# First head pair rotated on VectorE, float64 weight halves split 1024 columns at a time, and a newly planned issue order, in an attention + two-FFN kernel

## The chip, the cores and the metric

One core of a Trainium2 chip. The metric is the device time of one execution in microseconds (us); less is better. A time is the median of the runs shown.

## What is computed

Three steps in a row, all in float32:

```
q_rot, k_rot = rotate(q), rotate(k)                    # rotary embedding, B=2, H=8, S=576, D=64
attn = softmax(q_rot @ k_rot^T / sqrt(D));  x = attn @ v      -> 1152 tokens x 512
h = x @ w_in                                           # 512 -> 2048, w_in and w_out are float64
g = where(h >= 1, h, where(h <= -1, 0, (h + 1)^2 / 4)); y = g @ w_out    # 2048 -> 512
out = sum over 4 experts e of  p[:, e] * (relu(y @ w1[e]) @ w2[e])       # 512 -> 1024 -> 512
```

where `p` is `domain_probs` divided by its row sum.

## The kernel before

**Precision.** TensorE works on fp32r. Every float32 operand is split into a high part (a cast, "h") and a low part (value minus high, "l"), and each product is three matmuls: h·h, h·l, l·h.

**Stages.** Heads are taken two at a time: 8 pairs. Tokens of a pair lie in nine slots of 64 values (slots 0 to 4 and 4 to 8 are its two heads), so a whole q or k of a pair is a tile of 128 x 576. For each pair: loads by SyncE (SP), rotation (`rope`: two multiplications with the cos and sin planes of `tabs` and an addition, L894, L898, L902), the split (`split_h` L907, `split_l` L941), transposes on TensorE (`tr`, `k_first`) with copies back, then nine tiles of 128 queries with scores (`sc`, L1073/L1083), row maximum (DVE, L1090), exponential (ACT, L1095), transposes of the probabilities, product with v (`av`), and at last XH and XL, the split and transposed attention output (L1202, L1206). In the first pair everything is done in pieces (`k_first`, and `rope` with slots 0:2, 2:5, 5:9), so that scores can begin early. The first-pair rotations of q's slots 2:5 and 5:9 are on POOL and those of k and of q's slots 0:2 on DVE.

FFN1 runs over 4 chunks c of 512 hidden columns and 3 blocks b of 384 tokens: `in_unit` (L446 matmuls into `pi`, ACT relu and square, DVE `hb = max(min(.))` at L470, ACT and POOL splits) and `out_unit` (L498, added into ACC on DVE at L510). The float64 weights of a chunk come as raw 32-bit words, 1 MB per load, two loads for `w_in` and two for `w_out`, into two slots in turn. `w_split` (L360) turns one 512-column quarter into h and l: |high word| on ACT (L412), clamp, shift-and-mask, and-or on DVE (L402, L403, L404), low bits and or on DVE (L408, L409), h on ACT (L416), l on DVE (L417). A 1 MB load feeds two such jobs. The first chunk (c = 0) is converted during attention; 24 jobs for c = 1 to 3 follow, in the planned order among the units.

FFN2 runs in seven-product blocks of a Strassen-like scheme (L700, L709) and L733.

**Order.** Nothing is scheduled on the chip. Each operation is recorded by `op` with its engine, an estimated duration and a priority (the numbers in `CFG["o"]`, of which "a0" to "a9" and "f1" to "f5" belong to the first pair). `Plan.order` (L170) simulates a list schedule with them and the result is the order in which each engine's instructions are issued; each engine then runs its own list strictly in order and waits by semaphores.

Of the kernel before, what the change touches and what calls it, by code (L numbers as in the profile page):

```python
# [18 lines left out]
P = 128  # L19
# [67 lines left out]
SEARCH_FLAGS = [("rp", 8), ("ev", 9), ("evu", 3), ("ord0", 0), ("xe", 2), ("he", 2)]  # L87
# [45 lines left out]
class Plan:  # L133


    LAT = {"PE": 205.0, "ACT": 150.0, "DVE": 125.0, "POOL": 125.0, "SP": 100.0}
    ENTER, LEAVE, STALL = 95.0, 130.0, 105.0
# [32 lines left out]
    def order(self):  # L170
        prio = {o: o.prio for o in self.ops}
        free, ready, left = {}, {}, {}
        for o in self.ops:
            free.setdefault(o.eng, 0.0)
# [111 lines left out]
def fused_kernel(ctx: ExitStack, tc, q, k, v, w_in, w_out, dprobs, w1, w2, tab, out):  # L286
# [73 lines left out]
    def w_split(c, kind, a, prio, phase, slot, tmp, after=()):  # L360
# [45 lines left out]
        def c2():  # L406
# [5 lines left out]
        op("ACT", act_ns(512, True), prio, lambda: nc.scalar.activation(uy()[0], lohi()[1].bitcast(F32), AF.Abs),  # L412
           [rk], [uk], phase=phase)
        op("DVE", 2 * dve_ns(512, True) + dve_ns(512), prio, c1, [rk, uk], [uk, yk], phase=phase, port=True)
# [3 lines left out]
            l(), uy()[1], h().bitcast(F32), op=ALU.subtract), [yk, hk], [lk], wb, phase=phase, port=True)  # L418

# [110 lines left out]
    CT, TS = [], []  # L530
# [117 lines left out]
    def in2(c, u, pr):  # L648
# [152 lines left out]

    def load_part(t, src, b, hp, nm, j, eng="SP"):
# [13 lines left out]
    def plan_pair(n):  # L816
# [24 lines left out]
        def load(nm, j, pr, eng="SP"):  # L841
# [3 lines left out]
            else:  # L845
                op(eng, 650 if j == 2 else 480, pr, lambda: load_part(raws[nm](), src[nm], b, hp, nm, j, eng),
                   writes=[(raws[nm], j)], bufs=[raws[nm]], lat=2300.0)

        if first:
            def tload(a):  # L850
                if a == 0:
                    op("ACT", 700, -2000, lambda: None, writes=[("tab", 0)], lat=2300.0)
                    return
                op("SP", 650, -98, lambda: nc.sync.dma_start(tabs[:, :, 5:9], tab[:, :, 5:9]),
                   writes=[("tab", 1)], lat=3000.0)
            tload(0)
# [23 lines left out]
        def rope(x, eng, lo, hi, pr):  # L880
# [8 lines left out]
            tk = [("tab", z) for z, on in ((0, lo < 5), (1, hi > 5)) if on]  # L889
# [13 lines left out]
            op(engs[0], nss[0], pr, m1, rk + tk, sk, [raws[x], rot[x]], port=True)  # L903
            op(engs[1], nss[1], pr, m2, rk + tk, [(t2, lo)], [raws[x], t2], port=True)
# [86 lines left out]
        if first:  # L991
# [16 lines left out]
            rope("k", "DVE", 0, 5, -50)  # L1008
            rope("q", "DVE", 0, 2, O["a0"])
            split_h("k", 0, 5, -48)  # L1010
            split_h("q", 0, 2, O["a1"])
            split_l("k", 0, 5, O["a2"])
            k_first([(z, 0) for z in range(4)], [("ACT", K1, 0, 512, 0)], -46)
            k_first([(z, 1) for z in range(4)], [("DVE", K2, 0, 512, 0)], -45)
            split_l("q", 0, 2, O["a3"])
            k_first([(4, 0), (4, 1)], [("ACT", K1, 512, 640, 0), ("DVE", K2, 512, 640, 128)], -43)
# [6 lines left out]
            rope("k", "DVE", 5, 9, O["f1"])  # L1023
            rope("q", "POOL", 5, 9, O["f1"] + 0.2)
# [194 lines left out]
    def setup():  # L1219
        nc.scalar.dma_start(tabs[:, :, 0:5], tab[:, :, 0:5])  # L1220
# [52 lines left out]
    jobs = [(c, kind, a) for c in range(1, n1) for kind in range(2) for a in range(4)]  # L1273
# [66 lines left out]
    gate("gate_ts1", [("raw", 1), ("wtu", 1), ("wty", 1), ("ga", 2), ("gb", 2)])  # L1340
# [67 lines left out]
```

## Time and profile before

| | |
|---|---|
| median of 3 runs (range) | 772.02 us (769.37 to 772.02) |
| the profiled execution | 776.6 us |
| its span in the trace | 774.6 us |
| mean granted TensorE clock | 0.986 of full |
| PE busy | 737.4 us (95%) |
| DVE, ACT, POOL busy | 549.2, 353.7, 148.4 us |
| chain that ended last, by engine | PE 71%, DVE 18%, DMA 4%, ACT 3% |

The span is the time between the first and the last instruction in the trace, the execution's own time has about 2 us more around it. Busy times are those of the profiled execution, which lies 4.6 us above the median of the runs. PE is TensorE, DVE VectorE, ACT ScalarE, POOL GpSimd, SP SyncE; SPq is SP's work of issuing DMAs. A row of a timeline gives start, duration, engine, line, operation, output<-inputs, shape, count, and in brackets the idle time before it with what ended it.

### The profile page before, as it was taken

To read this page: it belongs to the slowest core of one execution; us is meant where nothing else is said; L and a number is where in the kernel's file an instruction comes from. 1 tells how busy PE (TensorE), PEld (TensorE's weight loads), DVE (VectorE), ACT (ScalarE), POOL (GpSimd) and SP (SyncE) were. 2 spreads that over 40 slices of the span, in tenths; PEclk is the share of its full clock that TensorE was granted. 3 is DMA by queue.
4 is the path that set the end of the run, shared out by engine and by line. 5 is a ranking of instruction groups with operands and counts; after the bars stand their busy time and mean duration, and the time that the engine had idled before them with its cause. 6 is when DMAs were issued, how large, how long until landed. Compare 5 with 4: busy or idle time off the path is not lost.

```text
span 774.6 us, 11850 instructions
## 1 busy us (share of the span) xinstructions
PE 737.4 (95%) x4507; PEld 664.9 (86%) x4507; DVE 549.2 (71%) x1057; ACT 353.7 (46%) x827; POOL 148.4 (19%) x145
## 2 busy tenths in 40 slices
PE   4888979999997989999999999999999999999998
PEld 3777757887997989999998899888998889898896
DVE  5978887787899997322698868386774858658462
ACT  3678667885656555434552333132432314223110
POOL 3867553212222223323420000000000000000000
PEclk9899999999998999999999999999999999999999
DMA  6344433223333331000101111110111101111002
GB/s 173 93 107 107 137 94 101 60 86 98 118 127 110 109 108 55 1 1 1 55 1 55 55 55 56 54 55 1 55 55 55 55 1 55 55 55 55 1 28 95
DMA packets 38984, 51.11 MB, mean 66 GB/s; under 512 B 7624, under 2 KB 22544, under 8 KB 38928
## 3 DMA queue, kind: packets, MB, share of 16 engines
q1 hardware_dynamic: 38254, 49.87, 20.7%
q8 instruction: 35, 0.57, 0.3%
q10 hardware_dynamic: 674, 0.49, 0.2%
q14 instruction: 21, 0.17, 0.1%
HBM read 43.60 MB, written 2.40 MB: 59 GB/s over the span
## 4 chain that ended last, share of the span: by engine, by line
PE 71%; DVE 18%; DMA 4%; ACT 3%; issue 2%; POOL 0%; SPq 0%; DVEq 0%; ACTq 0%; POOLq 0%
PE po L733 24%; PE q L700 20%; PE po L498 8%; PE pi L446 7%; PE av L1184 4%; PE sc L1073 3%; PE pt L1108 3%; DVE nm L1090 2%; DVE w L417 1%; DVE ts L409 1%; DVE ct L709 1%; ACT E L1095 1%; DMA wrawa<-in_moe_w_out_dram 1%; PE sc L1083 1%; DVE hb L409 1%
## 5 line engine op out<-in xcount | busy, mean ns | idle before, releaser
L709 DVE TENSOR_TENSOR ct<-q,ct 128x256 f32<-128x256 f32 (+1 forms) x224 | 92.7, 448 | 31.1 <-PE q L700 31.0
L733 PE MATMUL po<-w,ha 128*128 128x512 f32 x320 | 100.4, 394 | 0.0
L748 DVE SCALAR_TENSOR_TENSOR ACC<-po,ptile,ACC 128x512 f32<-128x512 f32 x63 | 46.1, 747 | 73.7 <-PE po L733 73.7
L733 PE MATMUL po<-w,hid1h 128*128 128x512 f32 x256 | 79.8, 393 | 0.0
L733 PEld LDWEIGHTS po<-w,ha 128*128 128x128 f32 x320 | 59.3, 187 | 13.9
L1090 DVE TENSOR_REDUCE nm<-sc 128x1 f32<-128x576 f32 x72 | 52.9, 749 | 16.0 <-PE sc L1073 8.5
L733 PE MATMUL po<-w,hb 128*128 128x512 f32 x160 | 63.1, 394 | 0.0
L1095 ACT ACTIVATE E<-sc,nm 128x576 f32<-128x576 f32 x72 | 53.9, 750 | 19.0 <-DVE nm L1090 13.0
L700 PE MATMUL q<-XH,w 128*128 128x256 f32 (+1 forms) x272 | 59.5, 293 | 0.0
L1073 PE MATMUL sc<-K,Q 128*128 128x288 f32 x256 | 50.4, 326 | 9.3 <-ACT E L1095 9.3
L446 PE MATMUL pi<-XH,w 128*128 128x384 f32 x192 | 52.0, 347 | 5.0 <-DVE hb L470 5.0
L733 PEld LDWEIGHTS po<-w,hid1h 128*128 128x128 f32 x256 | 47.2, 188 | 10.7 <-DVE ACC L748 1.6
L1073 PEld LDWEIGHTS sc<-K,Q 128*128 128x128 f32 x256 | 38.7, 200 | 14.4 <-ACT E L1095 13.3
L589 ACT CAST w<-wrawa 128x512 fp32r<-128x512 f32 x32 | 18.5, 620 | 70.0 <-PE po L733 69.1
L733 PE MATMUL po<-w,hid1l 128*128 128x512 f32 x128 | 50.0, 391 | 0.0
L683 ACT ACTIVATE ha<-ct 128x320 fp32r<-128x320 f32 x64 | 28.9, 472 | 43.0 <-DVE ct L709 42.9
L700 PE MATMUL q<-ts,w 128*128 128x256 f32 (+1 forms) x312 | 46.0, 296 | 0.0
L700 PEld LDWEIGHTS q<-XH,w 128*128 128x128 f32 x272 | 45.5, 188 | 0.4
L1108 PE MATMUL pt<-ident,E 128*128 128x128 f32 x288 | 41.3, 283 | 3.3 <-DVE PT L1054 2.9
L700 PEld LDWEIGHTS q<-ts,w 128*128 128x128 f32 x312 | 43.2, 189 | 0.2
L683 ACT ACTIVATE hid1h<-ct 128x256 fp32r<-128x256 f32 x64 | 24.8, 418 | 38.0 <-DVE ct L709 38.0
L446 PEld LDWEIGHTS pi<-XH,w 128*128 128x128 f32 x192 | 36.3, 196 | 5.7 <-DVE hb L470 5.7
(194 smaller groups left out, 1830.7 us busy)
## 6 DMA issues: line engine op xcount, KB each, us to landing
wrawa<-in_moe_w_dram SPq DMA_DIRECT2D x16, 1024.0 KB
wrawa<-in_moe_w_in_dram SPq DMA_DIRECT2D x5, 1024.0 KB
wrawa<-in_moe_w_out_dram SPq DMA_DIRECT2D x5, 1024.0 KB
K<-K SPq DMA_DIRECT2D x14, 304.0 KB
ts<-in_moe_w_in_dram SPq DMA_DIRECT2D x3, 1024.0 KB
ts<-in_moe_w_out_dram SPq DMA_DIRECT2D x3, 1024.0 KB
rawk<-in_k_dram SPq DMA_DIRECT2D x16, 128.0 KB
RV<-in_v_dram SPq DMA_DIRECT2D x16, 128.0 KB
```

The lines of the kernel that those rows point to most:

```text
L446: nc.tensor.matmul(ps()[:, 0:384], w[:, kt * P:(kt + 1) * P], x[:, kt, cols], start=(kt == 0 and m == 0), stop=(kt == 3 and m == 2))
L498: nc.tensor.matmul(ps()[:, 0:N], lh, rh, start=(kt == 0 and m == 0), stop=(kt == 3 and m == 2))
L683: op("ACT", act_ns(n, port), pr, lambda: nc.scalar.activation(hv(0), src(), AF.Relu), rk + gates[0], [hk], bufs, phase=1)
L700: nc.tensor.matmul(ps()[:, 0:n], w[x][:, kt, a * P:(a + 1) * P], r[y][:, kt, :], start=(kt == 0 and m == 0), stop=(kt == 1 and m == 2))
L709: nc.vector.tensor_tensor(ct(a, j), psv(), ct(a, i), op=ALU.add)
L733: nc.tensor.matmul(ps()[:], x[y], w[z], start=(kt == 0 and m == 0), stop=(kt == 3 and m == 2))
L748: op("DVE", 665, pr, lambda acc=acc, ps=ps, t=t: nc.vector.scalar_tensor_tensor(acc(), ps()[:], pt[:, t, e:e + 1], acc(), op0=ALU.mult, op ...
L1073: nc.tensor.matmul(sc()[:, a, 0:288], lh, KK()[:, c0:c0 + 288], start=(x == 0), stop=(x == 1))
L1090: op("DVE", 665, g0 + O["max"], lambda: nc.vector.tensor_reduce(nm(), pv(), axis=AX.XY, op=ALU.max, negate=True), [sc], [nm], [sc, nm])
L1095: nc.scalar.activation(Et()[:, o0:o0 + 576].rearrange("p (a c) -> p a c", a=2), pv(), AF.Exp, bias=nm(), scale=1.0, accum_out=sm()[:, s:s ...
L1108: nc.tensor.transpose(ps()[:, t * P:(t + 1) * P], Et()[:, c0 + t * P:c0 + (t + 1) * P], ident)
L1184: nc.tensor.matmul(pa()[64 * j:64 * j + 64, 0:N], lh, rh, start=(t == 0), stop=(t == 4))
```

## The change

1. **First pair.** `CFG["r0"] = 15`: all three pieces of q's rotation go to DVE, beside k's, which stay there. The first pair's operations get set priorities (k's at -6000 to -5960, q's by new numbers), which rank ahead of everything else.
2. **Tables.** Slots 5:9 of the cos and sin tables equal slots 0:4. Only slots 0:5 are loaded, as two DMAs of 160 KB (one per plane) on ACT's queue; before, 320 KB came on ACT's queue and 256 KB (slots 5:9) on SP's. ACT copies slots 0:4 to 5:9 for the later pairs, and the first pair's rotation of slots 5:9 reads slots 0:4.
3. **Weights.** `w_split2` converts what one 1 MB load brings, 1024 columns, in one job: |high word| and h on ACT at 1024 (h of `w_out` 2 x 512), on DVE three tensor-scalar operations (L441, L443, L445), one and-or (L448), one or (L451) at 1024, and l at 1024 (`w_in`, L462) or 2 x 512 (`w_out`, L471). So 12 jobs take the place of 24. The first chunk keeps `w_split`.
4. **Order.** New numbers for all priorities and for which engine takes which cast (`xe`, `he`, `rp`), query tiles of the first pair in the order 0, 2, 1, 5, 3, 4, 7, 6, 8 (before 3, 0, 4, 5, 1, 2, 6, 7, 8), and a few changed cost estimates in the planner. They alter which instruction follows which, and, for some casts of the rotated q and k, the engine.

```diff
 CFG = {
-    ... "ord0": [3, 0, 4, 5, 1, 2, 6, 7, 8], ...
+    "r0": 15, ... "ord0": [0, 2, 1, 5, 3, 4, 7, 6, 8], ...
-        "a0": 22.24, "a1": 3188.18, ...
+        "a0": -5515.81, "a1": -9498.77, ...
+    START = {"SP": 740.0, "ACT": 740.0}
...
+    def w_split2(c, kind, half, prio, slot, tmp):
...
+        op("ACT", act_ns(1024, True) + 80, prio, lambda: nc.scalar.activation(uy()[0], lohi()[1].bitcast(F32), AF.Abs),
+           [rk], [uk], phase=1)
+        add(dve_ns(1024, True), lambda: nc.vector.tensor_scalar(
+            uy()[1].bitcast(U32), lohi()[0], 2.0 ** -29, 7.0, op0=ALU.mult, op1=ALU.min), [rk], [yk])
+        add(dve_ns(1024, True), lambda: nc.vector.tensor_scalar(
+            uy()[0], uy()[0], F64_MIN, F64_MAX, op0=ALU.max, op1=ALU.min), [], [uk])
+        add(dve_ns(1024, True), lambda: nc.vector.tensor_scalar(
+            uy()[0].bitcast(U32), uy()[0].bitcast(U32), 3, 0x3FFFFFFF, op0=ALU.logical_shift_left, op1=ALU.bitwise_and),
+            [], [uk])
+        add(dve_ns(1024), lambda: nc.vector.scalar_tensor_tensor(
+            uy()[0].bitcast(U32), lohi()[1], 0xC0000000, uy()[0].bitcast(U32), op0=ALU.bitwise_and, op1=ALU.bitwise_or),
+            [rk], [uk])
+        add(dve_ns(1024), lambda: nc.vector.tensor_tensor(
+            uy()[1].bitcast(U32), uy()[1].bitcast(U32), uy()[0].bitcast(U32), op=ALU.bitwise_or), [uk], [yk])
...
         if first:
             def tload(a):
-                if a == 0:
-                    op("ACT", 700, -2000, lambda: None, writes=[("tab", 0)], lat=2300.0)
-                    return
-                op("SP", 650, -98, lambda: nc.sync.dma_start(tabs[:, :, 5:9], tab[:, :, 5:9]),
-                   writes=[("tab", 1)], lat=3000.0)
+                op("ACT", 650, -2000 + a, lambda: nc.scalar.dma_start(tabs[:, a, 0:5], tab[:, a, 0:5]),
+                   writes=[("tab", 0, a)], lat=FIRST_LAT)
...
+            op("ACT", act_ns(512, True), O["tb"], lambda: nc.scalar.copy(tabs[:, :, 5:9], tabs[:, :, 0:4]),
+               [("tab", 0, 0), ("tab", 0, 1)], [("tab", 1, 0), ("tab", 1, 1)])
...
+            t0 = 0 if first and lo == 5 else lo
+            t1 = t0 + hi - lo
...
-            rope("k", "DVE", 0, 5, -50)
-            rope("q", "DVE", 0, 2, O["a0"])
+            rope("k", "DVE", 0, 5, -6000)
+            r0 = ["DVE" if CFG["r0"] >> z & 1 else "POOL" for z in range(4)]
+            rope("q", r0[0], 0, 2, O["a0"])
...
-            rope("q", "POOL", 2, 5, O["a5"])
+            rope("q", r0[1], 2, 5, O["a5"])
...
-    jobs = [(c, kind, a) for c in range(1, n1) for kind in range(2) for a in range(4)]
+    jobs = [(c, kind, a) for c in range(1, n1) for kind in range(2) for a in range(2 if wide else 4)]
```

How the instructions stand now, at two places. First DVE at the start of the program, where t1, t2 are the rotation's results, raw the loaded q or k, and hl the split parts. Before (the first q piece stands behind all of k; q's slots 2:5 and 5:9 are on POOL):

```order
L894 TENSOR_TENSOR t1k_120<-rawk_109,tabs 128x320
L898 TENSOR_TENSOR t2k_124<-rawk_109,tabs 128x320
L894 TENSOR_TENSOR t1k_120<-rawk_109,tabs 128x256
L898 TENSOR_TENSOR t2k_124<-rawk_109,tabs 128x256
L941 TENSOR_TENSOR hlq_first<-t1q_126,hlq_first 128x3x64
L902 TENSOR_TENSOR t1k_120<-t1k_120,t2k_124 128x256
L917 CAST hlk_first<-t1k_120 128x4x64
L941 TENSOR_TENSOR hlk_first<-t1k_120,hlk_first 128x4x64
L902 TENSOR_TENSOR t1k_120<-t1k_120,t2k_124 128x320
L941 TENSOR_TENSOR hlq_first<-t1q_126,hlq_first 128x4x64
L917 CAST hlk_first<-t1k_120 128x5x64
L894 TENSOR_TENSOR t1q_126<-rawq_112,tabs 128x128
```

Of the change (the same first four rows, then both k additions, one cast, and these):

```order
L953 TENSOR_TENSOR t1q_141<-rawq_114,tabs 128x128
L957 TENSOR_TENSOR t2q_144<-rawq_114,tabs 128x128
L953 TENSOR_TENSOR t1q_141<-rawq_114,tabs 128x256
L961 TENSOR_TENSOR t1q_141<-t1q_141,t2q_144 128x128
L957 TENSOR_TENSOR t2q_144<-rawq_114,tabs 128x256
L1000 TENSOR_TENSOR hlk_first<-t1k_126,hlk_first 128x5x64
L961 TENSOR_TENSOR t1q_141<-t1q_141,t2q_144 128x256
L1000 TENSOR_TENSOR hlq_first<-t1q_141,hlq_first 128x2x64
L953 TENSOR_TENSOR t1q_141<-rawq_114,tabs 128x192
L957 TENSOR_TENSOR t2q_144<-rawq_114,tabs 128x192
L1000 TENSOR_TENSOR hlq_first<-t1q_141,hlq_first 128x4x64
L961 TENSOR_TENSOR t1q_141<-t1q_141,t2q_144 128x192
```

The whole rotation of q now stands on DVE, ahead of k's second cast, and POOL's list begins with the second pair's q.

Second, DVE in FFN1, where `w_in` of chunk 2 (w00h, w00l) is converted; `pi_0_x` are the results of the in-unit of chunk 1, block 0, and `hb` and `ts` are buffers that hold words on their way or hidden values. Before:

```order
L408 TENSOR_SCALAR hb_65<-ts_2553 128x512
L409 TENSOR_TENSOR hb_65<-hb_65 128x512
L470 SCALAR_TENSOR_TENSOR hb_65<-hb_65,pi_0_0_2943 128x384
L470 SCALAR_TENSOR_TENSOR hb_65<-hb_65,pi_0_1_2964 128x384
L417 TENSOR_TENSOR w00l<-hb_65,w00h 128x512
L402 TENSOR_SCALAR ts_2553<-ts_2553 128x512
L403 TENSOR_SCALAR ts_2553<-ts_2553 128x512
L404 SCALAR_TENSOR_TENSOR ts_2553<-wrawa,ts_2553 128x512
L470 SCALAR_TENSOR_TENSOR ts_2553<-ts_2553,pi_0_2_2986 128x384
L470 SCALAR_TENSOR_TENSOR hb_65<-hb_65,pi_0_3_3009 128x384
```

Of the change:

```order
L441 TENSOR_SCALAR ts_2579<-ts_2579 128x1024
L443 TENSOR_SCALAR ts_2579<-ts_2579 128x1024
L445 TENSOR_SCALAR ts_2579<-ts_2579 128x1024
L462 TENSOR_TENSOR w00l<-ts_2579,w00h 128x1024
L448 SCALAR_TENSOR_TENSOR ts_2579<-ts_2579 128x1024
L451 TENSOR_TENSOR ts_2579<-ts_2579 128x1024
L441 TENSOR_SCALAR ts_2579<-wrawa 128x1024
L443 TENSOR_SCALAR ts_2579<-ts_2579 128x1024
L525 SCALAR_TENSOR_TENSOR hb_65<-hb_65,pi_0_0_2909 128x384
L462 TENSOR_TENSOR w00l<-ts_2579,w00h 128x1024
L445 TENSOR_SCALAR ts_2579<-ts_2579 128x1024
L525 SCALAR_TENSOR_TENSOR hb_65<-hb_65,pi_0_1_2925 128x384
```

The operations are the same by kind, in pieces twice as long; the hidden-value operation (L470, now L525) stands between pieces of another job, as before.

## Rows read from the trace of the kernel before

**Rows 1.** Windows by stage: length, busy times, granted clock, DMA share.

```profile
core 0: us, PE busy (x) PEld busy (x) DVE busy (x) ACT busy (x) POOL busy (x), PEclk, DMA share, GB/s
0.00:18.50 18.50, 7.75 (x37) 5.57 (x37) 9.78 (x24) 5.74 (x15) 6.11 (x19) 1.00 0.60 166
18.50:35.00 16.50, 14.44 (x89) 12.56 (x89) 14.77 (x21) 11.52 (x32) 12.23 (x9) 0.79 0.43 114
35.00:122.00 87.00, 76.67 (x579) 61.46 (x579) 72.64 (x123) 60.19 (x179) 53.70 (x45) 0.96 0.38 101
122.00:189.50 67.50, 65.03 (x496) 52.55 (x494) 53.37 (x99) 52.47 (x147) 15.25 (x17) 1.00 0.29 77
189.50:237.90 48.40, 48.40 (x278) 47.80 (x276) 40.84 (x76) 29.85 (x60) 10.55 (x10) 1.00 0.42 143
237.90:292.00 54.10, 46.99 (x254) 46.35 (x255) 51.07 (x86) 31.48 (x60) 14.70 (x13) 0.94 0.31 104
292.00:774.60 482.60, 478.11 (x2784) 438.64 (x2782) 306.75 (x632) 162.47 (x338) 35.84 (x33) 1.00 0.12 41
```

**Rows 2.** Waits of 190 to 300 us: sum, times, longest.

```profile
PE pi L446 <- DVE hb L470: 7.1, 3, 4.2
```

**Rows 3.** Timeline of DVE and PE at the start of the program.

```profile
6.16 0.49 DVE L894 TENSOR_TENSOR t1k<-rawk,tabs 128x320 f32<-128x320 f32 x1 [4.24 <-DMA rawk<-in_k_dram]
...
8.35 0.43 DVE L894 TENSOR_TENSOR t1k<-rawk,tabs 128x256 f32<-128x256 f32 x1 [1.29 <-DMA tabs<-in_tab_dram]
...
14.86 0.28 DVE L894 TENSOR_TENSOR t1q<-rawq,tabs 128x128 f32<-128x128 f32 x1
...
18.57 2.55 PE L1073 MATMUL sc<-K,Q 128*128 128x288 f32 x8
```

**Rows 4.** Timeline of SP and POOL: the second pair's q.

```profile
15.81 0.88 SPq L806 DMA_DIRECT2D rawq<-in_q_dram  x2
...
21.41 1.41 POOL L894 TENSOR_TENSOR t1q<-rawq,tabs 128x576 f32<-128x576 f32 x1 [8.44 <-DMA rawq<-in_q_dram]
...
31.33 1.41 POOL L941 TENSOR_TENSOR hlq<-t1q,hlq 128x576 fp32r<-128x576 f32 x1 [0.53 <-PE pu L1134]
```

**Rows 5.** Timeline of DVE in FFN1.

```profile
195.26 0.43 DVE L402 TENSOR_SCALAR ts<-ts 128x512 f32<-128x512 f32 x1 [1.62 <-ACT ts L412]
...
205.55 0.43 DVE L403 TENSOR_SCALAR ts<-ts 128x512 uint32<-128x512 uint32 x1
206.01 0.69 DVE L404 SCALAR_TENSOR_TENSOR ts<-ts 128x512 uint32<-128x512 uint32 x1
206.62 0.42 DVE L402 TENSOR_SCALAR hb<-hb 128x512 f32<-128x512 f32 x1
...
241.46 1.01 DVE L470 SCALAR_TENSOR_TENSOR hb<-hb,pi 128x384 f32<-128x384 f32 x2
```

**Rows 6.** Timeline of PE in FFN1: the longest of its three waits.

```profile
242.06 0.69 PE L446 MATMUL pi<-XH,w 128*128 128x384 f32 x1 [4.17 <-DVE hb L470]
```

**Rows 7.** One-input DVE operation at two sizes: min/median/max ns, first and last start.

```profile
L929 DVE CAST hlq<-t1q x7: 384/416/1189, 29.9 to 144.6; 128x512 fp32r<-128x512 f32 x7
L930 DVE CAST hlq<-t1q x7: 182/186/189, 31.0 to 145.0; 128x64 fp32r<-128x64 f32 x7
```

**Rows 8.** The same cast on ACT at full size, columns as in rows 7.

```profile
L924 ACT CAST hlk<-t1k x2: 708/725/742, 55.0 to 133.6; 128x576 fp32r<-128x576 f32 x2
```

**Rows 9.** Timeline of SP: a lone 1 MB weight load, and an earlier one of two.

```profile
187.21 0.59 SPq L357 DMA_DIRECT2D wrawa<-in_moe_w_in_dram  x1
...
203.08 0.37 SPq L357 DMA_DIRECT2D wrawa<-in_moe_w_out_dram  x1
```

**Rows 10.** Windows of 2 us: length, granted clock, DMA share, GB/s.

```profile
205.00:207.00 2.00, 1.00 0.99 408
207.00:209.00 2.00, 1.00 0.17 68
```

**Rows 11.** Timeline of ACT: the first reading of the earlier load.

```profile
194.57 0.66 ACT L412 ACTIVATE ts<-wrawa 128x512 f32<-128x512 f32 x1
```

More of the change, by code (lines that the diff above doesn't have):

```diff
@@ L173, in order @@
         for o in self.ops:
-            free.setdefault(o.eng, 0.0)
+            free.setdefault(o.eng, self.START.get(o.eng, 0.0))
             ready.setdefault(o.eng, [])
@@ L411, in w_split @@
         uk, yk = ("wtu", tmp), ("wty", tmp)
-        op("ACT", act_ns(512, True), prio, lambda: nc.scalar.activation(uy()[0], lohi()[1].bitcast(F32), AF.Abs),
+        op("ACT", act_ns(512, True) + 45, prio, lambda: nc.scalar.activation(uy()[0], lohi()[1].bitcast(F32), AF.Abs),
            [rk], [uk], phase=phase)
-        op("DVE", 2 * dve_ns(512, True) + dve_ns(512), prio, c1, [rk, uk], [uk, yk], phase=phase, port=True)
+        op("DVE", 2 * dve_ns(512, True) + dve_ns(512) + 266, prio, c1, [rk, uk], [uk, yk], phase=phase, port=True)
         op("DVE", dve_ns(512, True) + dve_ns(512) + 130, prio, c2, [rk], [uk, yk], phase=phase, port=True)
@@ L418, in w_split, with lohi, uy, add @@
             l(), uy()[1], h().bitcast(F32), op=ALU.subtract), [yk, hk], [lk], wb, phase=phase, port=True)
+    def w_split2(c, kind, half, prio, slot, tmp):
+        par = c % 2
+        rk = ("raw", slot)
+        uk, yk = ("wtu", 2 + tmp), ("wty", 2 + tmp)
+        pair = (2 * half, 2 * half + 1)
+        bufs = [z for a in pair for z in wbufs.get((c, kind, a), [])]
+        def lohi():
+            tv = WRAW[slot].bitcast(U32).rearrange("p (a f w) -> p a f w", a=4 if kind == 0 else 2, w=2)
+            return tv[:, :, :, 0], tv[:, :, :, 1]
+        def uy():
+            return [x.rearrange("p (a f) -> p a f", a=4 if kind == 0 else 2) for x in WIDE[tmp]]
+        def add(ns, fn, rd, wr):
+            op("DVE", ns, prio, fn, rd, wr, phase=1, port=True)
+        op("ACT", act_ns(1024, True) + 80, prio, lambda: nc.scalar.activation(uy()[0], lohi()[1].bitcast(F32), AF.Abs),
[12 more added lines that the diff above has]
+            uy()[1].bitcast(U32), uy()[1].bitcast(U32), uy()[0].bitcast(U32), op=ALU.bitwise_or), [uk], [yk])
+        hk, lk = [[("W", par, kind, a, x) for a in pair] for x in "hl"]
+        if kind == 0:
+            def part(x):
+                t = (W00, W10)[par][x][:, 2 * half:2 * half + 2, :]
+                return t.rearrange("p t (a f) -> p t a f", a=4)
+            def y():
+                return uy()[1].rearrange("p a (t f) -> p t a f", t=2)
+            op("ACT", act_ns(1024, True), prio, lambda: nc.scalar.copy(part(0), y()), [yk], hk, bufs, phase=1)
+            op("DVE", dve_ns(1024), prio, lambda: nc.vector.tensor_tensor(
+                part(1), y(), part(0).bitcast(F32), op=ALU.subtract), [yk] + hk, lk, bufs, phase=1, port=True)
+            return
+        for z, a in enumerate(pair):
+            def w(x, a=a):
+                return W[(par, kind, a)][x]()
+            op("ACT", act_ns(512, True), prio, lambda w=w, z=z: nc.scalar.copy(w(0), uy()[1][:, z, :]), [yk], [hk[z]],
+               wbufs.get((c, kind, a), []), phase=1)
+            op("DVE", dve_ns(512), prio, lambda w=w, z=z: nc.vector.tensor_tensor(
+                w(1), uy()[1][:, z, :], w(0).bitcast(F32), op=ALU.subtract), [yk, hk[z]], [lk[z]],
+                wbufs.get((c, kind, a), []), phase=1, port=True)
@@ L888, in rope @@
             t2 = t2s[x]
-            tk = [("tab", z) for z, on in ((0, lo < 5), (1, hi > 5)) if on]
+            tk = [[("tab", z, y) for z, on in ((0, lo < 5 or first), (1, hi > 5 and not first)) if on] for y in range(2)]
+            t0 = 0 if first and lo == 5 else lo
+            t1 = t0 + hi - lo
             rk = raw_keys(x, lo, hi)
@@ L1022, in plan_pair @@
             tr("q", 2, 5, O["a8"])
-            rope("k", "DVE", 5, 9, O["f1"])
-            rope("q", "POOL", 5, 9, O["f1"] + 0.2)
+            rope("k", r0[2], 5, 9, O["f1"])
+            rope("q", r0[3], 5, 9, O["f6"])
             split_h("k", 5, 9, O["f2"])
@@ L1290, in split_one @@
         c, kind, a = jobs.pop(0)
-        w_split(c, kind, a, pr, 1, where[(c, kind, a // 2)], n_tmp[0] % 2)
+        if wide:
+            w_split2(c, kind, a, pr, where[(c, kind, a)], n_tmp[0] % 2)
+        else:
+            w_split(c, kind, a, pr, 1, where[(c, kind, a // 2)], 0)
         n_tmp[0] += 1
-        if a == 3 or (a == 1 and is_wide(c)):
+        if a == 3 or wide:
             load_next(pr)
@@ L1339, in fused_kernel @@
     gate("gate_ha1", hids(0))
-    gate("gate_ts1", [("raw", 1), ("wtu", 1), ("wty", 1), ("ga", 2), ("gb", 2)])
+    gate("gate_ts1", [("raw", 1), ("wtu", 2), ("wty", 2), ("wtu", 3), ("wty", 3), ("ga", 2), ("gb", 2)])
     gate("gate_u0", hids(1))
```

59 lines of the change are left out of this document (31 added, 28 removed), and 11 rows, old and new, of the table CFG.

## Prediction, made before the changed kernel ran

> **What bounds the kernel now.** I read the windows by stage first. From 292 us to the end PE is busy 478.11 of 482.60 us at full clock [rows 1]; its work there is the same in both kernels, so nothing can be gained in that stretch. What can change is PE's idle time and its half-clock time before 292 us. Start (0 to 18.5): PE busy 7.75, that is 10.8 idle, all ahead of the first score matmul at 18.57 [rows 3]. First pair (18.5 to 35): 2.1 idle, and a mean clock of 0.79, that is (1 − 0.79) × 16.5 = 3.5 us lost. Rest of attention (35 to 189.5): 10.3 + 2.5 = 12.8 idle, clock 0.96 over the first 87. FFN1 to 237.9: none idle. FFN1 to 292: 7.1 idle, clock 0.94, that is 3.2 lost. The waits view names the owner of the 7.1: three waits of an in-unit for a hidden-value operation on DVE (L470), which frees the `pi` buffer; the longest is 4.2 [rows 2, 6]. There DVE, busy 51.07 of 54.10, is the bound [rows 1].
>
> **The change part by part.** Unit prices first. Two-input DVE: 0.69 us for 512 columns, but the next one starts 0.61 later [rows 5], so a start-to-start step is the duration less 0.08: 320 columns 0.41, 256 columns 0.35, 128 columns 0.20 [rows 3], 192 by the mean of its neighbours 0.27. Hidden-value operation: two in 1.01, so 0.47 a step [rows 5]. One-input: 0.46 a step for 512 (205.55 to 206.01). 1024 columns occur nowhere. Bounds for one-input: 0.92 (twice the step) above; below, the slope between 64 and 512 columns, (416 − 186)/448 = 0.51 ns a column [rows 7], so 0.46 + 512 × 0.51 ns = 0.72. I take 0.72, since a line through two sizes of a like operation is nearer to it than a doubling that adds no saving at all. Two-input: slope (0.61 − 0.20)/384 = 1.07 ns, so 0.61 + 0.53 = 1.14 (double: 1.22).
>
> *Start.* DVE's first instruction waits for k's load until 6.16 and the second part of k for the tables until 8.35 (1.29 of idle) [rows 3]; that second wait goes, because the tables it needs are already there. From 6.16 to the last reading of q's raw data the planned list has five steps at 320 columns (k's cast among them), six at 256, four at 128 and two at 192: 5 × 0.41 + 6 × 0.35 + 4 × 0.20 + 2 × 0.27 = 5.5, so 11.6. Behind it, up to the last K copy ahead of the first score: 256, 192, a 256 cast, a 512 copy, 192 and 128 columns: 0.35 + 0.27 + 0.35 + 0.61 + 0.27 + 0.20 = 2.05, so the first score at about 13.7. That is 4.9 earlier than 18.57. It is the upper bound. q's work (six operations on POOL before) is in this sum and no longer parallel to it; what it costs DVE is paid by the waits that DVE had before. The halved table traffic costs nothing: ACT's copy of the tables (512 columns) lies in ACT's idle time, of which there are 12.8 of 18.5 us [rows 1].
>
> What can eat it: the second pair. Its q is issued on SP at 15.81 and ends POOL's wait at 21.41 [rows 4]; SP has only one load less (about 0.6) and still the same weight load ahead of it. POOL then has seven operations of 1.41 in a row up to the low part of q, which started at 31.33, ended 32.74 and would end about 30.7: 2.0 earlier. If PE ran dry until that, only 2.0 of the 4.9 would stay (lower bound). But PE has the remaining tiles of pair 0 in between, and what is ahead stays ahead, since PE is idle only 10.3 of the following 87 us. I take −4.0, nearer to the upper end, since pair 1's q is needed only when pair 0's tiles run out.
>
> *FFN1.* Take DVE from the start of the stage (195.26) to the first hidden-value operation of chunk 1, that at which PE waits 4.17 (241.46, 46.2 later). Before: 12 conversions of 3 × 0.46 + 2 × 0.60 = 2.58, 11 low parts of 0.60, 7 hidden-value operations of 0.47: 40.9, the rest waits and stretched operations. Changed, by the planned list: 6 jobs of 3 × 0.72 + 2 × 1.14 = 4.44, three low parts of 1.14 and four of 0.60, two one-input steps of the next job, six hidden-value operations: 26.6 + 5.8 + 1.4 + 2.8 = 36.7. So −4.2. From there to the same operation of chunk 2: before 27 one-input, 27 two-input steps, 12 hidden-value and 8 ACC operations: 38.0; changed 15 × 0.72 + 13 × 1.14 + 4 × 0.60 + 11 × 0.47 + 8 × 0.47 = 37.0. So −1.0. DVE is the bound, so PE's waits shrink by 5.2 of their 7.1. With 0.92 for one-input the two would be −0.2 and +1.9: +1.7 in all, the lower bound; the upper bound is all 7.1 of idle and the 3.2 of half clock. ACT and POOL have room (31.48 and 14.70 of 54.10).
>
> A rule speaks against this. The Trainium skill, "VectorE: DVE Perf Modes", section "The TRN2 errata", gives for an SBUF operation on VectorE 58 cycles at 0.96 GHz on top of the columns. By it, an estimate, merging two operations saves only 0.06 us, where the rows give 0.20 for one-input (2 × 0.46 − 0.72) and 0.08 for two-input. By that figure the 30 merged pairs of the first stretch (18 one-input, 12 two-input) would save 1.8 in place of 4.6, and the FFN1 term would be about −2. The same section notes that a measured fixed term was nearer 150 cycles (0.16 us), which is what the cast's rows give: 186 ns − 64 × 0.51 ns = 153 ns [rows 7]. So I stay with the rows.
>
> *Rest of attention.* By the planned lists DVE has 267 operations for 266, ACT takes five 576-column casts more and two of XH less, POOL 84 for 91. An ACT cast is 0.73 [rows 8], on DVE 0.42 + 0.19 [rows 7]; ACT was busy 112.7 of 154.5 [rows 1], so 3 us more are covered there. If that cover were gone they would cost 3. The order of tiles changes throughout; the rows don't tell whether PE's 12.8 idle grow or shrink. I put it at 0, bounds −6.4 (half the idle goes) and +3.
>
> **Sum.** −4.0 − 5.2 = −9.2 against the profiled execution: 776.6 − 9.2 = 767.4. The runs' median lies at 772.02/776.6 = 0.994 of that execution, so 762.9, say 763. About 0.5% (3.9 us) is what a measurement of this kernel can tell from no change, so "faster" is below 768.2 and "slower" above 775.9.
>
> **The rivals.**
> - *A, the forecast:* 763, own range 759 to 767. Chance 0.42.
> - *B, the new order also halves the middle's idle time:* 761.0 × 0.994 = 756.5. For it: 12.8 of PE's 32.8 us of idle before 292 us are there, and the start changes what is ready. Against: nothing in the rows names a wait that goes. Chance 0.18.
> - *C, one of the two terms fails.* Start only: 772.6, so 768; FFN1 only: 771.4, so 767. A way for the start: PE finishes pair 0 earlier, waits for pair 1's q, and a further stretch at half clock follows, as one did in 18.5 to 35 (3.5 lost), which takes back nearly all of 4.0. The Trainium skill, "TensorE: Matmul & The Clock Gate", Part 1, "What's actually happening", says that idleness sends the array back to 1.2 GHz; the trace agrees in that the window with the 4.17 wait has the clock at 0.94. Chance 0.18, of which 0.11 ends as faster and 0.07 as no change.
> - *D, the change doesn't do what it says:* 1024 columns cost on one-input operations twice what 512 do, and the start gives only its 2.0: −2.0 + 1.7, so 776.3 and 771.6. For it: the low and high words lie strided in the raw load, unlike the cast's columns. Against: at 512 columns the conversion's 0.42 to 0.43 [rows 5] is hardly more than the cast's 0.416. Chance 0.11, no change.
> - *E, slower: the conversions wait for their loads.* A 1024-column job uses up a whole 1 MB load, where two jobs shared one. Two slots take turns; between the and-or that last reads a slot and what first needs its next load lie, by the planned list with the prices above, about 5.3 and 6.0 us in turn (with ACT's absolute value in between). A lone load issued at 203.08 keeps the DMA engines at work until shortly after 207 [rows 9, 10]: about 4.5 us, which is in time. Of two loads in flight the first, issued at 187.21, was read only at 194.57 [rows 9, 11]: up to 7.4 us. At that, DVE would wait 2.1 and 1.4 in turn, 3.5 for each of six pairs of jobs, 21 in all, and PE behind it: 776.6 − 9.2 + 21 = 788.4, so 784. It decides when a load lands later than 5.3 to 6.0 after its slot is free. Against: DMA share in the stage is 0.42 and 0.31 [rows 1]. Chance 0.11.
>
> **How the numbers follow.** Faster: A 0.42 + B 0.18 + C 0.11 = 0.71. Same: C 0.07 + D 0.11 = 0.18. Slower: E 0.11. The range takes in A, C, D and most of B: 752 to 773; left out are E and the far end of B.
>
> **What would show it.** First score at about 13.7; second pair's q on POOL no later than 21; no wait of DVE for tables. L443 at 1024 near 0.72 a step, not 0.92; L451 near 1.14. PE's waits for the hidden-value operation (now L525) about 2 in place of 7.1. Wrong if DVE waits for weight loads between conversions, if PE's idle time in 35 to 189.5 grows beyond 12.8 by several us, or if a half-clock stretch turns up behind the first pair.

## The result, and the profile after

The changed kernel takes **760.72 us** (median of 4 runs, 759.86 to 761.57) against 772.02 (4 runs, 769.37 to 772.34): ratio 0.986, 95% interval 0.984 to 0.989. That is 11.3 us less; 763 had been forecast.

The profiled execution of before (776.6) was a long one. A second profile of the same kernel, taken in the experiments (`before_again`, 772.84), lacks its half-clock stretches (18.5 to 25.3, and 3.4 us each at 100 and 117), so I compare with that one. First its windows, then those of the changed kernel, cut at the first score matmul, at pair 1's first score, at the last `av` and at the first matmul of FFN2's 2785 (columns as in [rows 1]):

```profile
core 0: us, PE busy (x) PEld busy (x) DVE busy (x) ACT busy (x) POOL busy (x), PEclk, DMA share, GB/s
0.00:18.70 18.70, 8.44 (x37) 6.16 (x37) 9.85 (x24) 5.99 (x15) 6.18 (x19) 1.00 0.61 166
18.70:35.60 16.90, 15.08 (x87) 13.27 (x87) 14.52 (x21) 11.36 (x30) 12.47 (x9) 1.00 0.42 109
35.60:184.40 148.80, 139.20 (x1076) 111.34 (x1074) 123.54 (x221) 112.72 (x325) 68.68 (x62) 1.00 0.34 94
184.40:287.50 103.10, 95.54 (x528) 94.32 (x529) 93.00 (x163) 62.21 (x122) 25.55 (x24) 0.97 0.36 122
287.50:770.70 483.20, 478.80 (x2785) 439.06 (x2784) 306.98 (x630) 161.41 (x337) 34.98 (x33) 1.00 0.12 40
```

```profile
0.00:13.40 13.40, 7.94 (x32) 6.11 (x33) 8.25 (x26) 5.42 (x13) 1.82 (x13) 0.90 0.50 130
13.40:34.00 20.60, 18.75 (x130) 15.32 (x129) 15.71 (x26) 16.09 (x45) 12.10 (x9) 0.90 0.45 129
34.00:182.40 148.40, 139.95 (x1063) 112.45 (x1063) 121.74 (x216) 113.05 (x321) 68.64 (x60) 1.00 0.37 103
182.40:275.70 93.30, 89.65 (x506) 88.99 (x505) 82.70 (x107) 59.34 (x102) 31.94 (x24) 0.98 0.40 136
275.70:758.10 482.40, 477.74 (x2785) 439.40 (x2784) 302.15 (x619) 161.39 (x334) 33.69 (x33) 1.00 0.11 38
```

Read the first two numbers of each row. PE's idle time (length less busy) falls from 10.3 to 5.5 in the start and from 7.6 to 3.7 in FFN1, stays at 1.8 in the first pair and goes from 9.6 to 8.5 in the rest of attention: 9.8 of the 12.6 us by which the spans differ. The last stage is the same, as forecast. The matmul counts show that work has moved: pair 0's stretch holds 43 matmuls more, FFN1's 22 fewer, so lengths alone mislead here.

Read PEclk as well. Both of the first two stretches have 0.90 in the changed kernel and 1.00 in that execution of before: TensorE runs at half clock (PEclk 0.50) from 10.6 to 17.4, here over 14 to 16 (length, granted clock, DMA share, GB/s).

```profile
14.00:16.00 2.00, 0.50 0.86 227
```

That loses (1 − 0.90) × 20.6 = 2.1 us behind the earlier first score. A second profile of the changed kernel (`after_again`) has the same stretch at 10.9 to 17.8. What brings it is not shown: PE idles 3.1 us ahead of 10.15 in the changed kernel, but 7.2 us ahead of 11.70 in `before_again`, which keeps the full clock.

The start, DVE, PE and POOL (answers to [rows 3, 4]):

```profile
5.73 0.49 DVE L953 TENSOR_TENSOR t1k<-rawk,tabs 128x320 f32<-128x320 f32 x1 [3.80 <-DMA RV<-in_v_dram]
...
6.54 0.42 DVE L953 TENSOR_TENSOR t1k<-rawk,tabs 128x256 f32<-128x256 f32 x1
...
13.44 1.29 PE L1133 MATMUL sc<-K,Q 128*128 128x288 f32 x4
...
20.34 1.41 POOL L953 TENSOR_TENSOR t1q<-rawq,tabs 128x576 f32<-128x576 f32 x1 [17.70 <-DVE nm L1150]
```

The 1.29 us wait for the second part of the tables is gone, and the first score comes at 13.44. The second pair's q starts on POOL only 1.1 earlier than before (at 21.00 in `after_again`).

PE's waits in FFN1 (answer to [rows 2]; `po` is what an out-unit's matmuls write), and the rows around the first of them, of SP, ACT and PE:

```profile
PE po L553 <- DVE hb L525: 2.1, 1, 2.1
PE pi L501 <- DVE hb L525: 1.5, 1, 1.5
```

```profile
182.58 0.40 SPq L359 DMA_DIRECT2D ts<-in_moe_w_in_dram  x1
...
187.82 1.12 ACT L439 ACTIVATE ts<-ts 128x1024 f32<-128x1024 f32 x1 [3.98 <-DMA ts<-in_moe_w_in_dram]
188.84 0.50 ACT L527 CAST hid1h<-hb 128x384 fp32r<-128x384 f32 x1
...
191.01 1.24 PE L553 MATMUL po<-ha,w 128*128 128x384 f32 x4 [2.11 <-DVE hb L525]
```

This wait is new. The second weight load, into the FFN's own pool, can only be issued when attention's tiles are free (182.58). It lands 5.2 us later. ACT's absolute value of it stands ahead of the casts of the hidden values on ACT, so ACT does nothing for 4.0 us. Then relu and square of the next hidden values come late on ACT, their DVE operation behind them, PE behind that. In this execution a stretch of half clock follows (191.5 to 194.9, the 0.98 of the window); in `after_again` PE waits the same 2.1 and no half clock follows.

And DVE's conversion steps (answer to [rows 5]):

```profile
195.48 0.68 DVE L443 TENSOR_SCALAR ts<-ts 128x1024 f32<-128x1024 f32 x1
196.08 1.21 DVE L451 TENSOR_TENSOR ts<-ts 128x1024 uint32<-128x1024 uint32 x1
197.21 0.68 DVE L445 TENSOR_SCALAR ts<-ts 128x1024 uint32<-128x1024 uint32 x1
197.93 1.23 DVE L448 SCALAR_TENSOR_TENSOR ts<-ts 128x1024 uint32<-128x1024 uint32 x1
```

A one-input operation takes 0.68, but what follows starts 0.60 later when it belongs to the other job (first pair of rows) and 0.72 later when it reads the result (second pair). The two-input L451 at 196.08 has the next one start 1.13 later; it is 1.25 where that reads the result:

```profile
220.03 1.22 DVE L448 SCALAR_TENSOR_TENSOR ts<-wrawa,ts 128x1024 uint32<-128x1024 uint32 x1
221.28 1.22 DVE L451 TENSOR_TENSOR ts<-ts 128x1024 uint32<-128x1024 uint32 x1
```

### The profile page after: what moved, and what is told of

Same layout as the page of the kernel before. It is cut to its first block, busy times and chain, and to the rows that moved or that the text cites. A ratio compares the mean times of both kernels' runs of the same rounds, so it can differ in the third digit from the quotient of the medians.

```text
span 758.1 us, 11759 instructions
## 1 busy us (share of the span) xinstructions
PE 734.0 (97%) x4510; PEld 662.3 (87%) x4510; DVE 530.5 (70%) x991; ACT 355.3 (47%) x813; POOL 148.2 (20%) x137
## 4 chain that ended last, share of the span: by engine, by line
PE 78%; DVE 11%; DMA 4%; ACT 2%; issue 2%; POOL 2%; SPq 1%; DVEq 0%; POOLq 0%
PE po L788 25%; PE q L755 20%; PE po L553 11%; PE pi L501 11%; PE av L1244 4%; PE sc L1133 3%; PE pt L1168 2%; DVE nm L1150 1%; DVE ct L764 1%; ACT E L1155 1%; DMA wrawa<-in_moe_w_dram 1%; DMA ts<-in_moe_w_in_dram 1%; DVE ts L448 1%; PE sc L1143 1%; DVE ts L451 0%
## 5 line engine op out<-in xcount | busy, mean ns | idle before, releaser
L644 ACT CAST w<-wrawa 128x512 fp32r<-128x512 f32 x32 | 18.5, 617 | 70.9 <-PE po L788 66.9
L525 DVE SCALAR_TENSOR_TENSOR hb<-hb,pi 128x384 f32<-128x384 f32 x34 | 18.7, 549 | 33.9 <-ACT hb L523 23.7
L738 ACT ACTIVATE hid1h<-ct 128x256 fp32r<-128x256 f32 x64 | 25.4, 418 | 36.1 <-DVE ct L764 36.1
L1168 PE MATMUL pt<-ident,E 128*128 128x128 f32 x288 | 38.7, 274 | 0.9 <-ACT E L1155 0.3
L565 DVE TENSOR_TENSOR ACC<-po,ACC 128x384 f32<-128x384 f32 x36 | 19.8, 554 | 26.0 <-PE po L553 26.0
L553 PE MATMUL po<-ha,w 128*128 128x384 f32 x192 | 35.9, 347 | 2.1 <-DVE hb L525 2.1
L553 PEld LDWEIGHTS po<-ha,w 128*128 128x128 f32 x192 | 34.9, 196 | 2.4 <-DVE hb L525 2.4
L767 ACT COPY ct<-q 128x256 f32<-128x256 f32 (+1 forms) x32 | 12.6, 398 | 51.6 <-PE q L755 51.6
L788 PEld LDWEIGHTS po<-w,hb 128*128 128x128 f32 x160 | 30.0, 187 | 7.4
```

The source lines that it names most:

```text
L553: nc.tensor.matmul(ps()[:, 0:N], lh, rh, start=(kt == 0 and m == 0), stop=(kt == 3 and m == 2))
L738: op("ACT", act_ns(n, port) + 20, pr, lambda: nc.scalar.activation(hv(0), src(), AF.Relu), rk + gates[0], [hk], bufs, phase=1)
L788: nc.tensor.matmul(ps()[:], x[y], w[z], start=(kt == 0 and m == 0), stop=(kt == 3 and m == 2))
L1168: nc.tensor.transpose(ps()[:, t * P:(t + 1) * P], Et()[:, c0 + t * P:c0 + (t + 1) * P], ident)
```

## The experiments

**What is normal for the kernel before.** `before_again`: the kernel before, unchanged.

> The kernel before, unchanged, once more with a profile, because the profiled execution shown so far (776.6) lies 4.6 us above the median of its runs. Theory: the two short half-clock stretches at 100 and 117 us (3.4 us each, mean clock 0.96 in 35 to 122) are what that execution had beyond the others; here the clock in 35 to 122 is 0.98 or more, the execution takes 769 to 773, and the waits in FFN1 are 7 us as before. Rival: the stretches belong to the kernel; they come again and the execution takes 775 to 777.

Measured: 772.84 with the clock at 1.00 up to 184 us; the two stretches belonged to that one execution. So did the half clock at 18.5 to 25.3, from which the prediction had its 3.5 us lost in the first pair. FFN1 is as it was:

```profile
PE pi L446 <- DVE hb L470: 7.6, 3, 4.1
```

**Which half carries it.** Two kernels with one half each, attention in exactly the order of the one or the other kernel.

`attn_after_ffn_before`:

```diff
-        w_split2(c, kind, a, pr, where[(c, kind, a)], n_tmp[0] % 2)
+        w_split(c, kind, a, pr, 1, where[(c, kind, a // 2)], n_tmp[0] % 2)
```

> The changed kernel with the conversion of the weights put back to 512 columns a job, attention in exactly the changed order. Theory: the two terms are separate, so this kernel lacks the 5.2 us of FFN1: about 766 (0.992 of the time before), PE waits of about 7 us for the hidden-value operation between 170 and 285 us. Rival: attention alone carries the gain: 761 (0.986). Other rival: the conversion alone carries it: 772.

`attn_before_ffn_after` is the reverse edit in the kernel before.

> The kernel before with the 1024-column conversion alone, attention in exactly the order before. Theory: 772 less 5.2, about 767 (0.993), PE waits for the hidden-value operation about 2 to 4 us in place of 7. Rival (attention carries the gain): 772. Other rival (the conversion alone carries it): 761.

Measured together, with before at 770.77: attention alone 764.56, −6.2 (0.992, 0.990 to 0.994); conversion alone 762.35, −8.4 (0.989, 0.987 to 0.991). Neither half carries it alone, so both rivals fall. But both halves are larger than forecast, and their sum, 14.6, is more than the change brought. The waits of the conversion alone:

```profile
PE pi L499 <- DVE hb L523: 1.3, 1, 1.3
```

1.3 in place of 7.6, no half clock in FFN1 (1.00 against 0.97 in the window, that is 3.1 us), and no wait on `po`. Attention alone has no wait on `po` either; its waits for `pi` are 5.8 in all. So the wait at 191 above comes only where the new order and the wide conversion are together.

**Is it the width?** `halves512`: every 1024-column DVE instruction of the conversion issued as two.

```diff
-        add(dve_ns(1024, True), lambda: nc.vector.tensor_scalar(
-            uy()[0], uy()[0], F64_MIN, F64_MAX, op0=ALU.max, op1=ALU.min), [], [uk])
+        def halves(f):
+            def go():
+                for z in range(2):
...
+        add(dve_ns(1024, True), halves(lambda lo, hi, u, y, uu, yu: nc.vector.tensor_scalar(
+            u, u, F64_MIN, F64_MAX, op0=ALU.max, op1=ALU.min)), [], [uk])
```

> The changed kernel, same order on every engine, but each 1024-column instruction of the conversion on DVE issued as two of 512 columns (ACT's stay whole). Theory (width is what pays): DVE has 0.20 more for each of 36 one-input and 0.08 for each of some 30 two-input pieces, 9.6 us over the stage, of which 5 reach PE: 765 to 767, PE waits for the hidden-value operation 7 to 9 us. Rival (the new order of the conversions pays, not the width): within 1 us of the changed kernel, 761.

Measured: 764.33 (0.992, 0.990 to 0.993), that is 2.7 to 3.6 above the two medians of the changed kernel (761.61, 760.72), which were not timed beside it, and about 4.2 by the ratios (0.992 against 0.986). The width pays. Of PE's waits the theory had 7 to 9 us; they are 5.5:

```profile
PE pi L513 <- DVE hb L537: 3.3, 4, 1.6
PE po L565 <- DVE hb L537: 2.2, 1, 2.2
```
Per instruction it is worth less than the theory had it:

```profile
195.29 0.75 DVE L455 TENSOR_SCALAR ts<-ts 128x512 uint32<-128x512 uint32 x2
195.96 2.11 DVE L458 SCALAR_TENSOR_TENSOR ts<-wrawa,ts 128x512 uint32<-128x512 uint32 x2
...
200.54 1.28 DVE L458 SCALAR_TENSOR_TENSOR ts<-ts 128x512 uint32<-128x512 uint32 x2
201.75 1.28 DVE L474 TENSOR_TENSOR w10l<-ts,w10h 128x512 fp32r<-128x512 f32 x2
```

Two one-input halves take 0.67 where one of 1024 takes 0.60, two two-input halves 1.21 against 1.14: 0.07 a pair for either. In the kernel before, two one-input operations took 2 × 0.46 = 0.92 [rows 5], since every one of them was followed by an operation that read its result. So of the 0.32 saved (0.92 to 0.60) width is 0.07; the other 0.25 comes from separate planning of the five steps, with two jobs interleaved. That this is a matter of reading the result I take from the rows (0.60 against 0.72 in one trace, here and in the conversion alone); no run changed it by itself. In time it doesn't show here either: `attn_after_ffn_before`, with neither the width nor the separate planning, took 764.56, and `halves512`, which keeps the planning and was timed beside it, 764.33. The waits for `pi` are shorter (3.3 against 5.8), but the 2.2 on `po` takes that back.

**What did the new wait cost?** `late_abs`:

```diff
-        op("SP", 450, prio, fn, writes=[("raw", slot)], lat=5000.0, phase=phase)
+        op("SP", 450, prio, fn, writes=[("raw", slot)], lat=10000.0 if (c, kind, half) == (1, 0, 1) else 5000.0, phase=phase)
```

> The changed kernel with one planner figure changed: the first load into the second raw slot is taken to land 10 us after its issue in place of 5, which puts ACT's absolute value of it (a wait of 4.0 us for that load at 183.8 to 187.8, with the casts of the hidden values queued behind it on ACT) behind those casts. Theory (the new attention order brings a new wait that takes back some 3.8 us: 2.1 of PE waiting for the hidden-value operation at 189 and 1.7 of the half-clock stretch behind it): 757 (0.981 of the time before), no PE wait near 189. Rival (the conversions come later by as much, and PE waits at 236 instead): 760 to 761.

Measured: 756.45 (0.978, 0.976 to 0.981). Because the kernel before, timed beside it, took 773.53, 1.5 to 2.8 more than the two other times (772.02, 770.77), it was run again beside the changed kernel:

> The changed kernel once more, as the measure for the three others on the same chip: 0.986 of the time before (0.984 to 0.989).

> The kernel of late_abs on the same chip as the changed kernel. Theory: 3.8 us below the changed kernel (2.1 of PE's wait at 189 and 1.7 of half clock behind it), so 756.5 to 757.5. Rival (the 6 us by which the two ratios differ come from the chip): within 1 us of the changed kernel.

Measured: changed kernel 761.61 (0.986, 0.984 to 0.988), `late_abs_again` **757.49** (0.981, 0.979 to 0.983): 4.1 less, 3.8 expected. In its trace ACT reads the load without a wait, behind the casts, and PE's waits are these:

```profile
190.65 1.14 ACT L439 ACTIVATE ts<-ts 128x1024 f32<-128x1024 f32 x1
```

```profile
PE pi L501 <- DVE hb L525: 1.1, 1, 1.1
```

PE's wait on `po` is gone and the one behind it is not longer, so the rival falls. How the 4.1 is made up was not as expected. In the changed kernel's profile beside it (`after_again`) no half clock follows the wait, but more waits stand behind it:

```profile
PE pi L501 <- DVE hb L525: 2.2, 2, 1.6
PE po L553 <- DVE hb L525: 2.1, 1, 2.1
PE pi L501 <- DVE ts L525: 0.5, 1, 0.5
```

That is 4.8 of waits against 1.1, or 3.7 of the 4.1; that the 2.1 and 1.7 of the theory add up to about the same is a coincidence. The total, −14.3 us, is now about the sum of the two halves (14.6). This kernel beats both.

**The parts of the start**, the changed kernel's order kept on every engine. `q_on_pool`:

```diff
+            if first and x == "q" and lo >= 2:
+                es = [nc.gpsimd] * 3
```

> The changed kernel, same order, but the rotation of q's slots 2:5 and 5:9 in the first pair issued on POOL, as before the change. Theory of the forecast (the place of q's rotation matters): POOL's six steps of 0.6 to 0.8 us end later than DVE's, first score 1 to 2 us later than 13.4, time 762 to 763. Rival (the tables' early arrival is what pays; POOL starts at about 6 and ends by 11, beside DVE): first score between 12.9 and 13.7, time within 1 us of the changed kernel, 761.

`full_tables` (and no copy on ACT):

```diff
+            op("SP", 0, -97.5, lambda: nc.sync.dma_start(tabs[:, :, 5:9], tab[:, :, 5:9]))
...
-            t0 = 0 if first and lo == 5 else lo
+            t0 = lo
```

> The changed kernel, same order, but slots 5:9 of the tables loaded (256 KB on SP, behind k's loads, as before the change) in place of the copy on ACT, and read by the first pair's rotation. Theory: DVE's second k piece waits for them, 1.3 to 2 us as before, the first score moves to 14.7 to 15.5, the end by a good half of that: 761.5 to 762.5. Rival (the load lands in time): as the changed kernel, first score 13.4, 761.

`slow_start`: both.

> The changed kernel, same order, with both parts of the start undone: q's slots 2:5 and 5:9 rotated on POOL, and slots 5:9 of the tables loaded on SP. Theory: first score at 15.5 to 17 (2 to 3.5 later), and half or more of it at the end, 762 to 764, 1.5 to 3 above the changed kernel on the same chip. Rival (pair 1 is bound by its own loads, so the early start gives nothing): within 0.7 of the changed kernel.

First score: changed kernel 12.8 to 13.4 in two executions, `q_on_pool` 14.5, `full_tables` 14.9, `slow_start` 15.6. With q on POOL, its six steps run from 7.92 and end at 12.5, where DVE's end at 11.8. DVE's own steps beside them are longer as well: a 128-column addition takes 0.77 (third row), where it takes 0.28 in the changed kernel. The full tables make DVE wait again:

```profile
7.92 0.73 POOL L955 TENSOR_TENSOR t1q<-rawq,tabs 128x256 f32<-128x256 f32 x1 [5.26 <-DMA RV<-in_v_dram]
...
11.64 0.86 POOL L963 TENSOR_TENSOR t1q<-t1q,t2q 128x192 f32<-128x192 f32 x1
...
9.55 0.77 DVE L963 TENSOR_TENSOR t1q<-t1q,t2q 128x128 f32<-128x128 f32 x1
```

```profile
7.96 0.43 DVE L954 TENSOR_TENSOR t1k<-rawk,tabs 128x256 f32<-128x256 f32 x1 [1.58 <-DMA tabs<-in_tab_dram]
```

```profile
15.59 1.29 PE L1136 MATMUL sc<-K,Q 128*128 128x288 f32 x4
```

Times: 762.56 (0.986, 0.983 to 0.988) and 763.06 (0.986, 0.983 to 0.989); the changed kernel wasn't timed beside them, and by their ratios they can't be told from it: each alone is inconclusive. Both together: 764.15 (0.990, 0.988 to 0.992) against 761.61 of the changed kernel beside it, 2.5 us, nearly all of the 2.2 to 2.8 by which the first score is later. So these two parts give 2.5.

**The first pair alone.** `first_pair_only`: first pair, tables and tile order of the change, all other numbers of the order and the 512-column conversion as before. The planner then orders everything else anew, so this is not one edit in a fixed order.

> The changed kernel's first pair (rotation on DVE, half the table loads, its priorities and tile order) with all other numbers of the order and the 512-column conversion as before. Theory: the start is worth 4.0, so 767 (0.995), first score at 13.4, and the other 2 us that the changed attention saved (6.2 in all) come from the rest of the order. Rival: the start carries all 6.2, 764.6 (0.992). Other rival: the early first score is lost again by pair 1, whose q comes no earlier, 770 to 772.

Measured: 781.25, 7.7 us slower than before (1.010, 1.007 to 1.012). None of the three numbers holds. The last rival is right in that the early start is lost again, but not in its reason. The first score is at 13.2, but (PE, DVE and POOL):

```profile
37.77 4.54 PE L1294 MATMUL av<-PT,RV 128*64 128x320 f32 x16 [5.33 <-DVE avx L1305]
...
44.25 1.32 PE L1183 MATMUL sc<-K,Q 128*128 128x288 f32 x8 [0.26 <-ACT Q L1078]
...
35.52 1.77 DVE L456 SCALAR_TENSOR_TENSOR hb<-wrawa,hb 128x512 uint32<-128x512 uint32 x1
37.21 0.41 DVE L1305 TENSOR_TENSOR avx<-av,rbs 128x256 f32<-128x256 f32 x1
...
33.76 1.44 POOL L1050 TENSOR_TENSOR hlq<-t1q,hlq 128x576 fp32r<-128x576 f32 x1 [0.19 <-DVE hlq L1039]
```

Pair 1's q is ready at 35.2, when POOL ends its low part. What PE waits 5.3 us for is DVE's `avx`, which reads the first product with v of pair 0 and frees its buffer for the second. On DVE it stands behind a weight conversion of the first chunk, whose and-or takes 1.77 here and 0.69 elsewhere [rows 5]; on PE pair 1's transposes and scores stand behind that second product. So the planned order holds PE up, not q. Pair 1 begins at 44.25, over 8 us later than before (35.6), with the clock at 0.85 from 13.1 to 44.2. In FFN1 a wait of 6.5 follows. With this one set of numbers the early start brings nothing; what follows it has to be ordered for it.

**Can pair 1 be had earlier?** `late_abs_q_first`: as `late_abs`, and SP issues the first 1 MB weight load behind pair 1's q.

```diff
+        sp = [o for o in seq_ops if o.eng == "SP" and o.ns]
+        i = next(i for i, o in enumerate(sp) if o.ns == 450)
+        seq_ops.remove(sp[i])
+        seq_ops.insert(seq_ops.index(sp[i + 3]) + 1, sp[i])
```

> late_abs with one DMA issued in another place: SP issues the first 1 MB weight load behind the second pair's q in place of ahead of it. Theory (the weight load holds up q, and q's chain on POOL is what pair 1 waits for): POOL's first operation at 18 to 18.5 in place of 20.3, pair 1's first score 1 to 2 us earlier than 34.1, the PE wait of 1.2 near 36 and the half-clock stretch behind it shorter or gone, time 1 to 3 us below late_abs. Rival (pair 1 waits for k's chain, or PE has other work there): POOL starts earlier, the time stays within 0.7.

Measured: 758.75 (0.984, 0.982 to 0.986), 1.3 above `late_abs_again`; the intervals overlap, so no gain is shown. Pair 1's first score comes at 36.3, later than the 34.9 there, and the half clock behind it stays (38.1 to 44.9, there 36.1 to 43.0). POOL, ACT and PE:

```profile
18.47 1.42 POOL L953 TENSOR_TENSOR t1q<-rawq,tabs 128x576 f32<-128x576 f32 x1 [15.81 <-ACT E L1155]
```

```profile
20.86 0.66 ACT L414 ACTIVATE hb<-wrawa 128x512 f32<-128x512 f32 x1 [2.54 <-DMA wrawa<-in_moe_w_in_dram]
```

```profile
22.29 0.79 PE L1133 MATMUL sc<-K,Q 128*128 128x288 f32 x4 [2.69 <-ACT E L1155]
```

POOL starts 2.7 earlier than in `late_abs_again` (21.18). But now the weights land later; ACT waits 2.54 for them (1.34 there) with an exponential queued behind, and PE waits for that. It is the new wait of FFN1 in small: an in-order ACT that stands before a DMA holds up what PE needs. Moving that read back as well wasn't tried.

## Why the prediction was right, and where it was not

The forecast of −9.2 came out near the −10.1 to −11.3 measured, but its terms did not. Both were too small, and a wait that it did not foresee took most of the difference back: that the total came so near is partly luck.

- *What bounds the kernel* held: nothing changed after FFN1, and the idle time of the start and of FFN1 is what fell. The 3.5 us of half clock in the first pair and the 0.96 behind it were that one execution's.
- *Start, −4.0.* The mechanism and its size up to the first score held: 13.44 for 13.7 (with DVE's first step at 5.73, where the sum had 6.16), no wait for tables, q on POOL at 20.34 for "no later than 21". What the sum had no term for is the half clock behind the first score, 2.1 us (it stands in `slow_start` too, at 9.4 to 19.7). The start's share at the end is known for two of its parts only: 2.5 together. The whole of attention is worth 6.2 by itself, against 4.0 + 0 in the sum. How the other 3.7 divide between the first pair's order and the rest stays open: `first_pair_only` does not tell, since its order lost more elsewhere than the start gave.
- *FFN1, −5.2.* Right in kind, too small: 8.4 alone. The term that failed is the one-input step at 1024 columns, 0.72. It is that where the next operation reads the result, but 0.60 in most places (24 of the 29 steps in FFN1 that nothing stretched). Over the 20 + 15 one-input steps of the two sums that is up to 4.2 us more, by arithmetic. The two-input step is 1.14 as forecast, though the slope of 1.07 ns gives 0.55 and 1.16. PE's waits for L525 are 3.6, of which 2.1 new, where about 2 had been forecast; the conversion alone has 1.3. And the half clock that follows a long wait went with the waits; I had put it into the upper bound alone. I had taken the 0.20 saved per one-input pair as the worth of width. That mixed two things: width is 0.07.
- *The Trainium skill's figure*, which I weighed and set aside ("VectorE: DVE Perf Modes", section "The TRN2 errata": 58 cycles on top of the columns, an estimate of 0.06 us saved by a merge), agrees with the 0.07 that `halves512` shows. By that figure, an estimate, the FFN1 term comes to about 0 with the prediction's own counts (steps of 0.86 and 1.16, so −1.0 and +1.3), not to the −2 stated there. As a figure for width it was right and my reading of the rows wrong; the larger gain came from elsewhere. The same section says that SBUF latency is exposed between instructions; here an instruction more costs 0.07 us, and 0.12 more where it reads the result of the one before.
- *Rival E* (conversions wait for their loads) was the right mechanism in a place I had not looked at: not in each of six pairs of jobs but once, on ACT, at the first load into the FFN's own pool. It cost 4.1. I had costed what is queued behind a wait on DVE; I should have asked the same for ACT's absolute value, which is the first reader of every load.
- *Rival C* (PE runs ahead of pair 1 and the clock falls) is near to what `first_pair_only` does, but there PE waits for DVE, with q ready. The half-clock stretch behind the first pair, named as a sign of being wrong, is not in the first profile of the changed kernel; in `after_again` it is (38.3 to 41.7, 1.7 us lost), behind a wait of 1.2 for an exponential, and the forecast held all the same.
- *Rivals B and D*: the idle time of the rest of attention went from 9.6 to 8.5, not to half; and 1024 columns cost 0.60 to 0.72, not 0.92.
- Together: −9.2, 3.2 more in FFN1 and 2.2 more in attention, 4.1 given back: −10.5. Not all of these parts were timed side by side, so this is an account and not a proof.

## What to carry to other kernels

Before you price a wider instruction, look in the trace at whether the old ones were followed by a reader of their result: interleaving two independent chains may bring more than the width (here 0.25 of 0.32 by the rows, though no run took it alone). For each load, name its first reader on an in-order engine and list what is queued behind it; a planner that takes a load's landing too early puts the reader in front of work that the critical engine needs. Two edits with separate places need not add up: run each half alone, and if the sum is larger than the whole, look for a wait that only the combination has.

## What was not expected of the hardware

A one-input DVE operation of 1024 columns has the next one start 0.60 us later, but 0.72 if that reads its result; a two-input one 1.14 and 1.25. At 512 columns the one-input step is 0.34 (half of 0.67, `halves512`) and 0.46 [rows 5]. A 128-column addition on DVE takes 0.77 beside POOL's rotation and 0.28 without it (`q_on_pool`). A 1 MB load took 5.2 us from its issue (182.58) to its first reading (187.82), where I had 4.5 from another one.
